# When a batch's router does its steps inside an attention unit: the gate products, one exponential, the last transposes

## The chip, the cores and the metric

The kernel runs on one core of one Trainium2 chip. The metric is the device time of one execution in microseconds (us). Before the change it is 1287.62 us, the median of three runs (1287.07 to 1288.91).

## The reference

Attention over 8 batches and 8 heads, whose queries are averaged in twos, and behind it a mixture of 8 experts, of which each token uses one.

```python
q_pool = q.reshape(8, 8, 576, 2, 64).mean(axis=3)           # q, k, v: (8, 8, 1152, 64)
scores = q_pool @ k.transpose(0, 1, 3, 2) / 8.0
attn = softmax(scores)                                      # 576 x 1152 for each head
x = (attn @ v).transpose(0, 2, 1, 3).reshape(4608, 512)
logits = x @ w_gate                                         # (4608, 8)
e_idx = argmax(logits, axis=1)
gate_w = softmax(logits)[e_idx]
eom = sigmoid(x @ w_output_gate)[e_idx]
out = gate_w * eom * (relu(x @ w1[e_idx]) @ w2[e_idx])      # w1: 512x1024, w2: 1024x512
```

## The kernel before

The attention works through 32 pairs, one pair being two heads of one batch, four pairs to a batch. A pair is cut into 11 units, named in `UNITS`: nine D units (two chunks of 128 keys against 512 queries) and two T units (numbers 4 and 10, the last 64 queries of one head against all keys). For each unit TensorE makes the scores (lines L396 and L397) into one of two PSUM tiles of two banks, `sps`. ScalarE exponentiates them twice: once into float16 (`ph`) and once into float32. The difference of the two, `pl`, is formed on GpSimd in the even units and on VectorE in the odd ones (L465), where the float32 exponential stands in `sps` itself. An odd unit's score tile is therefore free only when L465 has read it. Three units later TensorE multiplies `ph` and `pl` with the values (L479 to L481, tile `av`). Between these, TensorE makes products of the next pair's queries and keys (`mp`, L339; mostly two to a unit) whose row maxima VectorE reduces (`pm`, L341).

The `mp` products, the transposes and the router share three PSUM banks, handed out by `psum()`: the bank that has been free longest is next. A tile that asks with `hold` keeps its bank until `free`; meanwhile the `mp` products go round in two banks, and each has to wait until VectorE has read the one two before it.

The order on TensorE, VectorE, ScalarE and GpSimd is written out by hand; each engine does its instructions in the order in which the program issues them. The main loop issues a unit in this order: the pending L465 of the unit before; one step of every router generator (`step_routers(True)`); the unit's scores and their exponentials; then `mp` products and value products in turn. In units 2 and 8 of a pair, which `CLOSE` names by the unit whose values are due, three before (10 and 5), all value products come first, and behind them the normalisation of a finished head (`norm`, L520 to L522, which writes `xb`). Between the first and the second `mp` product of a D unit, `step_routers(False)` steps those generators again whose last yield was not a 1. So a `yield 1` says "next at the start of the next unit", and a bare `yield` says "next in the middle of this D unit, or at the start of the next unit, whichever comes first".

A router generator `logits(b, c, xb)` starts in unit 2 of the pair that follows the pair (b, c). It transposes the two heads' columns of `xb` on TensorE (L576) in two groups, of two and three blocks; ScalarE writes the float16 part `xTh` (L578), and VectorE the rest `xTl` (L580). For the last pair of a batch (c is 3) it goes on: `at(8)` yields 1 until unit 8, then come 60 small products with the gate weights (the burst, L591) into a held bank. `router` follows: two GpSimd iotas, the maximum and the expert's choice on VectorE (L607 to L611), then L615 and L617, the exponential of the logits on ScalarE (L619, tile `exg`), which frees the held bank, and `sums()`: a reduction on VectorE (L625), its exponential on ScalarE (L626) and another reduction (L630). From unit 2 of the next pair on the ranks and the scatter follow (L637 to L667).

A batch's router thus runs in the first pair of the next batch. There are seven such pairs, numbers 4, 8, 12, 16, 20, 24 and 28; they are called router pairs here, and the others ordinary pairs. The eighth batch's router runs behind the attention. "Unit 0" behind a router pair is that of the following pair. The experts' work (`Moe`, L1034 to L1107) comes after the attention.

Of the kernel before, what the change touches and what calls it, by code (L numbers as in the profile page):

```python
# [92 lines left out]
def attention(tc, qT, kT, vL, wg, keep, xrows, idscr, cum, pairs, setup, scat, init, exps, behind, presplit, lastav):  # L93
    nc = tc.nc
    nb = len(pairs) // 4
    with ExitStack() as ctx:
# [17 lines left out]
        def psum(hold=False, name="tp"):  # L114

            while len(held) == 3:
                pop() if fill else pendv.pop(0)()
            k = next(i for i in banks if i not in held)
            free(k)
            if hold:  # L120
                held.add(k)
            x = ps_m.tile([128, 512], F32, name=name, tag=f"mp{k}")
            return (x, k) if hold else x

        def free(k):
            held.discard(k)
            banks.remove(k)
            banks.append(k)
# [227 lines left out]
        def pop(k=1):  # L356
            while k and fill:
                fill.pop(0)()
                k -= 1
# [150 lines left out]
        def close(n, h):  # L510
            p = pairs[n]
            if p[0] not in xbs:
                xbs[p[0]] = sm.tile([128, 5, XW], F32, name="xb", bufs=2)
            xb = xbs[p[0]]
            av_ = avt[n, h][1]
            r = keep['rs'][:, 2 * n + h]
            H = 2 * p[1] + h

            def norm():
                nc.vector.tensor_scalar(out=r, in0=av_[:, :, 64], scalar1=1e-9 * math.exp(SHIFT), scalar2=VS / XS, op0=ALU.add, op1=ALU.mult)  # L520
                nc.vector.reciprocal(out=r, in_=r)
                nc.vector.tensor_tensor(out=xb[:, :, 64 * H:64 * H + 64], in0=av_[:, :, 0:64], in1=r.unsqueeze(2).broadcast_to([128, 5, 64]), op=ALU.mult)  # L522
                if h == 1:
                    routers.append([logits(p[0], p[1], xb), 0])
            fill.insert(0, norm)
# [4 lines left out]
        def at(k):  # L530
            while cur[0] != k:
                yield 1
# [34 lines left out]
        def logits(b, c, xb):  # L567

            yield 1
            if c < 3:  # L570
                yield 1
            for c0, c1, grp in ((0, 256, (0, 1)), (256, NQ, (2, 3, 4))):
                tx, tk = psum(True)
                for i, t in enumerate(grp):
                    r = 64 if t == 4 else 128
                    nc.tensor.transpose(out=tx[:, 128 * i:128 * i + r], in_=xb[0:r, t, 128 * c:128 * c + 128], identity=ident[0:r, 0:r])  # L576
                hi, lo = (x[:, c, c0:c1] for x in xT)
                nc.scalar.copy(out=hi, in_=tx[:, 0:c1 - c0])  # L578
                yield 1
                nc.vector.tensor_tensor(out=lo, in0=tx[:, 0:c1 - c0], in1=hi, op=ALU.subtract)  # L580
                free(tk)
            if c < 3:
                return
            if b < nb - 1:
                yield from at(8)
            pop(99)
            tl, tk = psum(True)
            ops = [(xT[i][:, c_], w[:, c_]) for c_ in range(4) for i, w in ((0, wh), (0, wl), (1, wh))]
            for t in range(5):
                for i, (x, w) in enumerate(ops):  # L590
                    mm = nc.tensor.matmul(tl[:, 16 * t:16 * t + 16], lhsT=x[:, 128 * t:128 * t + 128], rhs=w, start=i == 0, stop=i == len(ops) - 1)  # L591
            yield from router(b, xb, tl, tk, mm)
# [3 lines left out]
        def router(b, xb, tl, tk, lt):  # L596
# [18 lines left out]
            V.tensor_tensor(out=ohb, in0=em8, in1=b8(em), op=ALU.is_equal)  # L615
            so = sm.tile([128, 5, 8], F32, name="so", bufs=2)
            V.tensor_tensor(out=so, in0=og, in1=ohb, op=ALU.mult)  # L617
            ex = exg[b % 2]
            late.append(nc.scalar.activation(out=ex[:, :, 0:8], in_=g, func=AF.Exp, scale=1.0 / LSC))  # L619
            free(tk)  # L620
# [971 lines left out]
```

## Time and profile before

| | |
|---|---|
| Median of three runs | 1287.62 us |
| Profiled execution, its own time | 1290.03 us |
| Span of the program in that execution | 1288.2 us |
| Granted TensorE clock, mean | 0.996 |
| TensorE busy | 1214.6 us (94%) |
| VectorE busy | 1062.5 us (82%) |
| ScalarE busy | 1023.6 us (79%) |
| GpSimd busy | 856.8 us (67%) |

The profiled execution is 2.4 us above the median. Busy time is a sum over stages; the attention takes about the first 850 us of the span, the experts the rest. A busy TensorE is not one at its peak, since the ends of its matmuls are modelled.

### The profile page before, as it was taken

The numbers are of one execution on the slowest core, as the hardware profiler recorded it, in microseconds if no ns is written. First come the engines' busy times: TensorE is split into PE (matmuls) and PEld (weight loads), VectorE is DVE, ScalarE is ACT, GpSimd is POOL, SyncE is SP. The second block draws the span as 40 slices with busy tenths as digits, with TensorE's granted clock in tenths as the row PEclk, the third lists the DMA queues.
The fourth block names the chain that finished last, engine by engine and source line by source line (L and its number), as shares of the span: only waits on it lengthen the run. The fifth ranks groups of instructions, "written<-read, shape, count | busy, mean of one in ns | idle before, by whom it ended". The sixth has DMA issues, their size and how long they took to land.

```text
span 1288.2 us, 39248 instructions
## 1 busy us (share of the span) xinstructions
PE 1214.6 (94%) x15960; PEld 829.0 (64%) x15960; DVE 1062.5 (82%) x2149; ACT 1023.6 (79%) x1528; POOL 856.8 (67%) x709
## 2 busy tenths in 40 slices
PE   6999999899999999999999999899999999999996
PEld 3666656566666666666666666577676767666764
DVE  8898879788888888888888989887877676767886
ACT  6999889799899989989989889955656565656784
POOL 6988788789889879879879998536233333233421
PEclk9999999999999999999999999999999999999999
DMA  5455444345444445445545653079986767676850
GB/s 175 143 159 168 133 133 138 108 137 143 142 134 135 127 125 157 131 127 134 156 125 137 190 160 106 15 236 351 400 298 224 270 215 270 220 267 223 304 170 16
DMA packets 102209, 225.54 MB, mean 175 GB/s; under 512 B 18411, under 2 KB 33983, under 8 KB 102018
## 3 DMA queue, kind: packets, MB, share of 16 engines
q1 hardware_dynamic: 92114, 201.42, 49.8%
q0 software_dynamic: 9056, 20.85, 4.8%
q8 instruction: 127, 2.08, 0.7%
q10 hardware_dynamic: 848, 0.66, 0.2%
q14 instruction: 64, 0.52, 0.1%
HBM read 160.04 MB, written 22.50 MB: 142 GB/s over the span
## 4 chain that ended last, share of the span: by engine, by line
PE 55%; DVE 18%; ACT 12%; POOL 7%; issue 4%; DMA 3%; SPq 1%; ACTq 0%; DVEq 0%; POOLq 0%
PE hps L1053 14%; DVE pm L341 5%; PE sps L396 5%; PE yp L1092 5%; PE yp L1093 5%; PE sps L397 5%; DVE pl L465 5%; PE yp L1095 4%; PE mp L339 4%; ACT sps L461 4%; ACT ph L460 4%; PE av L481 3%; PE av L479 3%; PE av L480 3%; POOL pl L445 2%
## 5 line engine op out<-in xcount | busy, mean ns | idle before, releaser
L341 DVE TENSOR_REDUCE pm<-mp 128x1 f32<-128x512 f32 (+2 forms) x672 | 417.8, 663 | 28.3 <-PE mp L339 24.9
L445 POOL TENSOR_TENSOR pl<-p,ph 128x1024 f16<-128x1024 f32 x128 | 272.6, 2130 | 85.9 <-ACT ph L444 80.2
L396 PE MATMUL sps<-qa,ka 128*128 128x512 f16 (+2 forms) x1216 | 266.1, 280 | 8.0 <-DVE pl L465 7.3
L397 PE MATMUL sps<-qb,kb 65*128 65x512 f16 (+2 forms) x1216 | 266.8, 280 | 3.1 <-DMA qb<-mr 2.9
L479 PE MATMUL av<-vt,ph 128*128 128x65 f16 x2304 | 263.1, 193 | 3.3 <-DVE xb L522 3.2
L480 PE MATMUL av<-vt,ph 128*128 128x64 f16 x2304 | 263.6, 194 | 0.0
L481 PE MATMUL av<-vt,pl 128*128 128x65 f16 x2304 | 262.2, 193 | 1.1 <-issue 0.7
L479 PEld LDWEIGHTS <-ph 128*128 128x128 f16 x2304 | 215.4, 97 | 62.9 <-issue 24.0
L465 DVE TENSOR_TENSOR pl<-sps,ph 128x512 f16<-128x512 f32 x310 | 199.7, 686 | 61.2 <-ACT sps L461 54.8
L480 PEld LDWEIGHTS <-ph 128*128 128x128 f16 x2304 | 213.4, 97 | 40.3 <-issue 0.8
L339 PE MATMUL mp<-ka,qa 128*128 128x512 f16 (+1 forms) x768 | 203.9, 326 | 17.5 <-DVE pm L341 15.5
L481 PEld LDWEIGHTS <-pl 128*128 128x128 f16 x2304 | 214.0, 99 | 1.7 <-POOL pl L445 0.9
L1053 PE MATMUL hps<-x,w1h 128*128 128x256 f16 (+2 forms) x1408 | 207.1, 260 | 3.7 <-DVE x L1041 3.7
L1053 PE MATMUL hps<-x,w1l 128*128 128x256 f16 (+2 forms) x704 | 178.6, 260 | 0.0
L461 ACT ACTIVATE sps<-sps 128x1024 f32<-128x1024 f32 x155 | 159.8, 1031 | 1.0
L443 ACT ACTIVATE p<-sps 128x1024 f32<-128x1024 f32 (+1 forms) x160 | 140.8, 880 | 23.8 <-PE sps L397 14.6
L460 ACT ACTIVATE ph<-sps 128x1024 f16<-128x1024 f32 x124 | 128.1, 1033 | 23.4 <-PE sps L397 21.1
L1067 ACT ACTIVATE hh<-hps 128x512 f16<-128x512 f32 (+2 forms) x88 | 48.1, 548 | 119.4 <-PE hps L1053 118.1
L1053 PEld LDWEIGHTS <-w1h 128*128 128x128 f16 x1408 | 131.6, 98 | 15.4
L397 PEld LDWEIGHTS <-kb 65*128 65x128 f16 x1216 | 97.2, 97 | 58.6 <-issue 17.0
L444 ACT ACTIVATE ph<-sps 128x1024 f16<-128x1024 f32 x128 | 131.7, 1029 | 0.0
L396 PEld LDWEIGHTS <-ka 128*128 128x128 f16 x1216 | 98.3, 98 | 45.7 <-issue 3.9
(308 smaller groups left out, 2798.3 us busy)
## 6 DMA issues: line engine op xcount, KB each, us to landing
vp<-in_vL_dram SPq DMA_DIRECT2D x32, 576.0 KB
qp<-in_qT_dram SPq DMA_DIRECT2D x31, 576.0 KB
kpf<-in_kT_dram SPq DMA_DIRECT2D x31, 576.0 KB
ka<-xk SPq DMA_DIRECT2D x120, 144.0 KB
raw2a<-in_w_dram SPq DMA_DIRECT2D x16, 1024.0 KB
raw1b<-in_w_dram SPq DMA_DIRECT2D x14, 1024.0 KB
raw2b<-in_w_dram SPq DMA_DIRECT2D x14, 1024.0 KB
raw1c<-in_w_dram SPq DMA_DIRECT2D x14, 1024.0 KB
```

The costliest lines, as they stand in the source:

```text
L339: nc.tensor.matmul(mp[:, w * j:w * j + w], lhsT=l, rhs=r, start=True, stop=True)
L341: nc.vector.tensor_reduce(out=o, in_=mp[:, 0:w * len(ts)].rearrange("p (t k) -> p t k", t=len(ts)), axis=AX.X, op=ALU.max)
L396: for m in (nc.tensor.matmul(out, lhsT=st['ka'][:, h, ks], rhs=st['qa'][:, o + q0:o + q1], start=True, stop=False), nc.tensor.matmul(out, ...
L397: nc.tensor.matmul(out, lhsT=st['kb'][:, h, ks], rhs=st['qb'][:, h, q0:q1], start=False, stop=True)):
L445: nc.gpsimd.tensor_tensor(out=pl, in0=p32, in1=ph, op=ALU.subtract)
L460: ex(out=ph, in_=x)
L461: e_ = ex(out=x, in_=x)
L465: l = nc.vector.tensor_tensor(out=pl[:, j], in0=x[:, j], in1=ph[:, j], op=ALU.subtract)
L479: nc.tensor.matmul(o[:, 0:65], lhsT=hi, rhs=vt[:, h, c, 0:65], start=first, stop=False)
L480: nc.tensor.matmul(o[:, 0:64], lhsT=hi, rhs=vt[:, h, c, 66:130], start=False, stop=False)
L481: lastav[:] = [nc.tensor.matmul(o[:, 0:65], lhsT=lo, rhs=vt[:, h, c, 0:65], start=False, stop=last).ins]
L1053: d['mm'] = nc.tensor.matmul(hp[:, f, 0:w], lhsT=W1[l][g][:, c, fs], rhs=d['x'][:, c, o:o + w], start=c == 0 and i == 0, stop=c == 3 and i ...
```

## The change

Three lines are added to or altered in the two generators; all of them apply to the batches 0 to 6 only (`b < nb - 1`).

```diff
         def logits(b, c, xb):
             yield 1
-            if c < 3:
+            if c < 3 or b < nb - 1:
                 yield 1
...
             if b < nb - 1:
                 yield from at(8)
+                yield
             pop(99)
             tl, tk = psum(True)
...
             V.tensor_tensor(out=so, in0=og, in1=ohb, op=ALU.mult)
+            if b < nb - 1:
+                yield
             ex = exg[b % 2]
             late.append(nc.scalar.activation(out=ex[:, :, 0:8], in_=g, func=AF.Exp, scale=1.0 / LSC))
             free(tk)
```

The first puts the last pair's transposes of a batch at the starts of units 4 and 5, where those of the other three pairs are, in place of units 3 and 4. The second puts the burst and the two iotas in the middle of unit 8, between its two `mp` products and so behind its scores and value products, in place of its start. The steps behind it move along: L607 to L611 from the middle of unit 8 to the start of unit 9, L615 and L617 from the start to the middle of unit 9. The third puts L619 at the start of unit 10, behind unit 9's exponentials on ScalarE, in place of the start of unit 9. With it `sums()` (L625, L626, L630) goes from the middle of unit 9 to the start of unit 0 of the next pair, since unit 10 is a T unit and has no middle step. The ranks stay at unit 2.

## Rows read from the trace of the kernel before

**Rows 1.** The page, part 1: busy us, share of the span, instructions by engine.
```profile
PE 1214.6 (94%) x15960; PEld 829.0 (64%) x15960; DVE 1062.5 (82%) x2149; ACT 1023.6 (79%) x1528; POOL 856.8 (67%) x709
```
**Rows 2.** TensorE's waits, 100 to 840 us: total us, times, longest.
```profile
PE mp L339 <- DVE pm L341: 14.2, 31, 0.7
PE tp L576 <- DVE xb L522: 7.3, 7, 1.1
```
**Rows 3.** ScalarE's waits in the same stretch.
```profile
ACT exg L619 <- DVE so L617: 13.8, 7, 2.0
```
**Rows 4.** Stretches, ordinary and router pair: length, busy of PE, PEld, DVE, ACT, POOL, clock.
```profile
308.40:315.21 6.81, 6.76 (x120) 4.74 (x116) 6.21 (x13) 6.65 (x11) 5.55 (x5) 1.00 0.45 168
332.33:340.07 7.74, 6.69 (x119) 4.67 (x116) 6.06 (x12) 6.88 (x11) 6.30 (x6) 1.00 0.25 81
319.13:328.09 8.96, 8.58 (x150) 5.69 (x146) 8.36 (x19) 8.96 (x12) 7.74 (x6) 1.00 0.33 79
343.99:355.89 11.90, 10.29 (x209) 7.33 (x206) 9.26 (x26) 9.15 (x14) 7.63 (x7) 1.00 0.56 165
```
**Rows 5.** Timeline, TensorE, router pair 12: start, us, what, [idle before, releaser].
```profile
335.66 0.41 PE L576 MATMUL tp<-ident,xb 128*128 128x128 f32 x2 [1.05 <-DVE xb L522]
...
346.02 0.17 PE L591 MATMUL tp<-wh,xTh 128*128 128x16 f16 x1 [0.39 <-DVE pm L341]
...
347.53 0.38 PE L396 MATMUL sps<-qa,ka 128*128 128x512 f16 x1
...
351.35 0.38 PE L339 MATMUL mp<-ka,qa 128*128 128x512 f16 x1 [0.30 <-DVE pm L341]
...
352.76 0.38 PE L339 MATMUL mp<-ka,qa 128*128 128x512 f16 x1 [0.67 <-DVE pm L341]
...
355.89 0.38 PE L396 MATMUL sps<-qa,ka 128*128 128x512 f16 x1 [0.25 <-DVE pl L465]
```
**Rows 6.** Timeline, TensorE, ordinary pair 11 from unit 8 to unit 0.
```profile
321.04 0.38 PE L396 MATMUL sps<-qa,ka 128*128 128x512 f16 x1
...
323.10 0.59 PE L339 MATMUL mp<-ka,qa 128*128 128x512 f16 x2
323.53 0.38 PE L396 MATMUL sps<-qa,ka 128*128 128x512 f16 x1
...
327.50 0.39 PE L339 MATMUL mp<-ka,qa 128*128 128x128 f16 x4
...
328.09 0.38 PE L396 MATMUL sps<-qa,ka 128*128 128x512 f16 x1
```
**Rows 7.** Timeline, VectorE, units 8 to 10 of pair 11.
```profile
324.64 2.47 DVE L341 TENSOR_REDUCE pm<-mp 128x1 f32<-128x512 f32 x4
327.25 1.29 DVE L465 TENSOR_TENSOR pl<-sps,ph 128x512 f16<-128x512 f32 x2
```
**Rows 8.** Timeline, VectorE, unit 8's router steps in pair 12.
```profile
351.21 0.19 DVE L607 TENSOR_REDUCE mx<-tp 128x5 f32<-128x40 f32 x1
...
352.03 0.68 DVE L341 TENSOR_REDUCE pm<-mp 128x1 f32<-128x512 f32 x1
```
**Rows 9.** Timeline, ScalarE, units 9 and 10 of pair 12.
```profile
353.08 0.20 ACT L619 ACTIVATE exg<-tp 128x40 f32<-128x40 f32 x1 [1.97 <-DVE so L617]
353.18 1.02 ACT L460 ACTIVATE ph<-sps 128x1024 f16<-128x1024 f32 x1
...
355.02 0.20 ACT L626 ACTIVATE sl<-sl 128x5 f32<-128x5 f32 x1
```
**Rows 10.** Timeline, ScalarE, units 0 and 1 behind pair 11.
```profile
328.81 1.08 ACT L424 ACTIVATE p<-sps 128x512 f32<-128x512 f32 x2 [0.43 <-PE sps L397]
...
331.36 1.02 ACT L460 ACTIVATE ph<-sps 128x1024 f16<-128x1024 f32 x1 [0.56 <-PE sps L397]
```
**Rows 11.** Timeline, ScalarE and TensorE, units 4 and 5 of pair 6.
```profile
181.53 0.67 ACT L256 CAST xk<-kpf 128x576 f16<-128x576 f32 x1 [3.08 <-DMA kpf<-in_kT_dram]
...
185.09 0.50 PE L396 MATMUL sps<-qa,ka 128*128 128x512 f16 x1 [2.81 <-DVE pl L465]
```

## The prediction, made before the changed kernel ran

> **What bounds the kernel now.** I read the page first, then the waits of TensorE and ScalarE in the attention, then the lengths of matching stretches of a router pair and an ordinary pair, and last the timeline of both. The page has TensorE busy for 94% of the span, the other engines for 67% to 82% [rows 1]: time can be won only where TensorE stands still, or by taking work from it, and this change takes none. Its largest waits are `mp` products that wait for VectorE's maxima (14.2 us in 31 waits) and transposes that wait for `xb` (7.3 us in 7) [rows 2]. ScalarE waits 13.8 us for L617, also 7 times, once in each router pair [rows 3]. Seven is the number of router pairs.
>
> What this costs is seen in the stretches [rows 4]. From unit 2's first score product to unit 5's, ordinary pair 11 takes 6.81 us and router pair 12 takes 7.74, with the same TensorE work (6.76 and 6.69 busy): the same five transposes, standing elsewhere. From unit 7's first score product to unit 0's of the next pair they take 8.96 and 11.90 us. In pair 11's stretch TensorE is busy 8.58 of 8.96 us, so this is nearly its floor. The router's own TensorE work there is the burst, 346.02 to 347.53, that is 1.51 us [rows 5]. The excess is therefore 0.93 us in the first stretch and 11.90 - 8.96 - 1.51 = 1.43 us in the second, and the timeline shows where it lies: 1.05 us before the transposes, 0.39 before the burst, 0.30 and 0.67 before unit 9's `mp` products, 0.25 before unit 0's scores [rows 5].
>
> **The change part by part.** *Transposes a unit later.* They are moved to where the other three pairs have theirs; five transposes, two casts and two subtractions go along, all issued in the same order as there. `xb` is then written long before. Pair 11 is the picture of it, so the stretch should take 6.81: -0.93 us. No DMA is moved, and `at(8)` still finds the transposed data two units old.
>
> *Burst behind unit 8's scores.* I lay pair 11's times out from unit 8's first score product, t = 0 at 321.04 [rows 6], and put 1.51 us in. The first `mp` product stands at 2.06 and the second at about 2.3, so the burst runs from 2.3 to 3.8; unit 9's scores move from 2.49 to 4.00, unit 10's last `mp` product from 6.46 to 7.97, unit 0's scores from 7.05 to 8.56. Does anything then wait? VectorE starts the four maxima of units 8 and 9 at 3.60, 0.60 apart (2.47 us for four of 0.68) [rows 7]; the burst does not hold them, since the first needs only the product at 2.06. Unit 8's two are done at 4.88. L607 to L611 took 0.82 us from the first to the next maximum [rows 8], and are free to start, the burst being over: 4.80 to 5.62. Unit 9's first maximum runs to 6.30; L615 and L617, at the same 0.2 us each, to 6.63; unit 9's second to 7.31. Unit 9's scores are four products, 1.01 us by the 0.38 of one and the 0.59 of two [rows 6], and complete at 5.01; its two exponentials take 1.94 us on ScalarE (from L619 to L626) [rows 9], to 6.95. L465 can start at 7.23, VectorE's next turn, and its first half, half of 1.29 us, is read at 7.9. Unit 0's scores want that at 8.56: 0.65 us to spare. The bank that the burst holds is now held until unit 10, so the products of units 9 and 10 go round in two banks. Each needs the maximum two products before. Unit 9's first, four products of 0.21 behind 4.00, stands at 4.85 and needs the one that ends at 4.28: 0.57 us to spare. Unit 10's last, at 7.97, needs the one that ends at 7.31: 0.66. The two between have about 1 us. So the stretch should take 8.96 + 1.51 = 10.47: -1.43 us. The iotas are two short GpSimd instructions on an engine at 67%, wanted a pair later: nothing.
>
> *Exponential behind unit 9's.* L619 finds its input long there, and its 1.97 us of idle time [rows 9] goes. That time is not counted again: it is part of why L465, and with it unit 0's scores, came late.
>
> *`sums()` at unit 0.* This is the new wait, and the diff does not show it. L626 now stands on ScalarE ahead of unit 0's exponentials and waits for L625, which stands on VectorE behind both maxima of unit 10. VectorE: L465 until 8.52, the maxima until 9.72, L625 until 9.83. L626 runs at 9.87, the exponentials behind it from 9.97. Pair 11 has them 0.72 us behind the scores (328.81 against 328.09) [rows 6, 10], which would be 9.28. So 0.69 us of hold. Unit 1's exponentials, next on ScalarE, have 0.56 us of idle time before them in pair 11 [rows 10], which swallows most: 0.13 us is left, and passes through unit 1's L465 to unit 3. From below the cost is nothing; a gain is excluded, for no engine is given work earlier. From above I take a hold as long as L619's 1.97 us, and of the longest hold in the trace, 3.08 us on a late load, all but 0.27 us came out on TensorE (2.81) [rows 11]: 1.70 us. I take 0.13, since its terms are rows of just this place.
>
> *Sum.* Per router pair -0.93 - 1.43 + 0.13 = -2.23 us, and seven of them -15.6 us. The profiled execution took 1290.03 us, so its like after the change takes 1274.4. It lies 2.4 us above the median of the runs, and on the median of 1287.62 the sum gives **1272.0 us**. Behind the attention nothing is altered, so the experts start as much earlier as the attention ends.
>
> **The rivals.** *First: the hold at unit 0 takes back most of it.* VectorE is nearly always busy in units 8 to 10 (8.36 of 8.96 us even in pair 11 [rows 4]), and if it comes to L625 1.3 us later than I have it, the hold is as long as L619's and costs 1.70 us: -0.66 us a pair, 4.6 in all, 1283.0 us. Against it: the burst gives VectorE 1.51 us in which TensorE feeds it nothing. The Trainium skill ("TensorE: Matmul & The Clock Gate", under the engine queue depths) has ScalarE's and VectorE's queues as strictly first in, first out. The trace agrees: L460, whose scores were long there, ran right behind L619 and its 1.97 us [rows 9]. By that rule the hold cannot be passed; could it be, the sum would be 7 x 2.36 = 16.5 us less.
>
> *Second: the burst only changes its place.* The waits behind the burst [rows 5] come back in units 9 and 10, because VectorE still has the same eight small steps to fit in. Then only the transposes pay: -0.93 + 0.13 a pair, 5.6 in all, 1282.0 us. For it speaks that VectorE's work is the same; against it that these steps were pushed together before, because `norm` and unit 8's maxima had to wait for products that stood behind the burst; now the value products and the first `mp` product stand ahead of it.
>
> *Third, slower: the bank.* It is held from the middle of unit 8 to unit 10, so four `mp` products go round in two banks where two did. If VectorE runs 1.3 us later than laid out, each of the four waits as the worst did, 0.67 us [rows 5], and unit 0's scores wait their 0.25 again: 2.93 us a pair, against 2.23 won. That is +0.70 us, 4.9 in all, 1292.5 us. It decides from the point where the spare 0.57 us is used up, and makes the kernel slower once the four lose 2.23. Against it: two of the four have about 1 us to spare. The Trainium skill ("Trainium Kernel Development and Optimization", Best Practices) says that bubbles which recur can mean that PSUM ran out; the 0.30 and 0.67 in every router pair agree with it, and by it alone this change, which holds the bank longer, would lose.
>
> **How the numbers follow.** The forecast has 0.76, the first rival 0.10, the second 0.09, the third 0.05. The range is 1267 to 1282 us: its lower end is the sum without any hold (16.5 us, 1271.1) less some 4 us, since a late load as that of 3.08 us [rows 11] may fall elsewhere or nowhere; its upper end reaches to the second rival. What one measurement of this kernel can tell from no change is about 0.2%, 2.6 us: forecast and the first two rivals lie beyond it. Faster 0.93; within 0.2%, 0.03, from the near parts of the second and third; slower 0.04.
>
> **What would show it.** The waits of L576 for `xb` should be gone, and unit 2 to unit 5 take 6.8 us in router pairs. The burst should start behind unit 8's first `mp` product without a wait and unit 9's scores come 4.0 us behind unit 8's; L619 should have no idle time before it; unit 7 to unit 0 should take some 10.5 us. ScalarE should stand idle some 1.1 us before L626 (the 0.43 that pair 11 has there [rows 10] and the 0.69), and unit 1's exponentials should follow with almost no gap. I am wrong if L339 or unit 0's scores wait in units 9 and 10, if L626's idle time is near 2 us and unit 3's scores wait for L465, or if the seven pairs gain and the loads of the pairs behind them come later by as much.

## The result, and the profile after

The changed kernel took 1268.71 us (median of 4 runs, 1266.22 to 1271.5), the kernel before 1287.34 us in the same rounds (4 runs, 1284.13 to 1288.91). The ratio is 0.9858, with a 95% interval of 0.9839 to 0.9876: 18.6 us less, where 15.6 were forecast. The profiled execution took 1269.41 us; its span is 1267.7 us, against 1290.03 and 1288.2 before. Lines of the code up to 585 keep their numbers; the burst's L591 is now L592, L607 is L608, L617 is L618, L619 is L622, L625 and L626 are L628 and L629.

The page of the kernel after, part 1, against [rows 1]. TensorE's work is the same to 0.5% (1214.6 to 1209.3 us), its instructions the same in number; what went is time between them.

```profile
PE 1209.3 (95%) x15960; PEld 827.6 (65%) x15960; DVE 1060.0 (84%) x2149; ACT 1023.1 (81%) x1528; POOL 856.3 (68%) x709
```

The waits of the kernel after, 100 to 840 us (total, times, longest), against [rows 2, 3]:

```profile
PE mp L339 <- DVE pm L341: 9.3, 17, 0.8
...
ACT sl L629 <- DVE sl L628: 9.3, 7, 1.4
...
ACT xk L256 <- DMA kpf<-in_kT_dram: 3.4, 3, 1.6
...
ACT exg L622 <- DVE so L618: 2.8, 2, 2.4
...
PE sps L397 <- DMA qb<-mr: 1.5, 3, 0.8
```

The transposes' seven waits for `xb` are gone, 14 of the 31 waits of the `mp` products too. ScalarE's seven waits at the exponential of the logits are down to two, and seven new ones stand at L629, the second ScalarE step of `sums()`. The stretches of router pair 12, unit 2 to unit 5 and unit 7 to unit 0, as in [rows 4]:

```profile
321.30:328.10 6.80, 6.75 (x120) 4.73 (x116) 6.19 (x13) 6.64 (x11) 5.45 (x5) 1.00 0.25 89
332.02:342.11 10.09, 9.75 (x210) 7.20 (x207) 9.48 (x25) 9.25 (x13) 8.13 (x8) 1.00 0.42 93
```

7.74 became 6.80, and 11.90 became 10.09 us, 0.4 below the 10.47 forecast. TensorE's timeline of that router pair, units 8 to 10, and its only waits from unit 8's scores to unit 3 of the next pair, the two in the last lines:

```profile
333.94 0.38 PE L396 MATMUL sps<-qa,ka 128*128 128x512 f16 x1
...
336.00 0.38 PE L339 MATMUL mp<-ka,qa 128*128 128x512 f16 x1
336.21 0.17 PE L592 MATMUL tp<-wh,xTh 128*128 128x16 f16 x1
...
337.94 0.38 PE L396 MATMUL sps<-qa,ka 128*128 128x512 f16 x1
...
338.81 0.38 PE L339 MATMUL mp<-ka,qa 128*128 128x512 f16 x1
339.02 0.19 PE L479 MATMUL av<-vt,ph 128*128 128x65 f16 x1
...
339.36 0.19 PE L481 MATMUL av<-vt,pl 128*128 128x65 f16 x1
339.39 0.38 PE L339 MATMUL mp<-ka,qa 128*128 128x512 f16 x1
...
342.11 0.38 PE L396 MATMUL sps<-qa,ka 128*128 128x512 f16 x1
...
350.48 0.38 PE L339 MATMUL mp<-ka,qa 128*128 128x512 f16 x1 [0.82 <-DVE pm L341]
...
351.65 0.38 PE L339 MATMUL mp<-ka,qa 128*128 128x512 f16 x1 [0.43 <-DVE pm L341]
```

The burst starts 0.21 us behind unit 8's first `mp` product, without a wait; unit 9's scores come 4.00 us behind unit 8's (333.94 to 337.94). None of the five waits of [rows 5] is left; one that the kernel before does not have stands just ahead of unit 8's scores (told of at e1). ScalarE in the same place, and into the next pair:

```profile
340.92 0.20 ACT L622 ACTIVATE exg<-tp 128x40 f32<-128x40 f32 x1
...
343.69 0.21 ACT L629 ACTIVATE sl<-sl 128x5 f32<-128x5 f32 x1 [1.31 <-DVE sl L628]
343.81 1.07 ACT L424 ACTIVATE p<-sps 128x512 f32<-128x512 f32 x2
...
345.67 1.04 ACT L460 ACTIVATE ph<-sps 128x1024 f16<-128x1024 f32 x1
```

L622 has no idle time, where L619 had 1.97 [rows 9]. L629 stands idle 1.31 us ahead of unit 0's exponentials, forecast at some 1.1, and unit 1's (345.67) follow with no gap, where pair 11 had 0.56 [rows 10].

### The profile page after: what moved, and what is told of

Read it like the earlier page. It is cut to its first block, busy times and chain, and to the rows that moved or that the text cites. A ratio compares the mean times of both kernels' runs of the same rounds, so it can differ in the third digit from the quotient of the medians.

```text
span 1267.7 us, 39249 instructions
## 1 busy us (share of the span) xinstructions
PE 1209.3 (95%) x15960; PEld 827.6 (65%) x15960; DVE 1060.0 (84%) x2149; ACT 1023.1 (81%) x1528; POOL 856.3 (68%) x709
## 4 chain that ended last, share of the span: by engine, by line
PE 55%; DVE 18%; ACT 12%; POOL 8%; issue 5%; DMA 2%; SPq 1%; DVEq 0%; POOLq 0%; ACTq 0%
PE hps L1056 15%; PE yp L1095 5%; PE yp L1096 5%; PE sps L396 5%; DVE pm L341 5%; DVE pl L465 5%; PE yp L1098 4%; PE sps L397 4%; PE mp L339 4%; ACT sps L461 4%; ACT ph L460 4%; PE av L481 3%; PE av L480 3%; PE av L479 3%; ACT ph L444 2%
## 5 line engine op out<-in xcount | busy, mean ns | idle before, releaser
L341 DVE TENSOR_REDUCE pm<-mp 128x1 f32<-128x512 f32 (+2 forms) x672 | 416.2, 662 | 25.4 <-PE mp L339 24.2
L465 DVE TENSOR_TENSOR pl<-sps,ph 128x512 f16<-128x512 f32 x310 | 199.5, 685 | 53.5 <-ACT sps L461 49.6
```

What stands on the lines that cost most here:

```text
L341: nc.vector.tensor_reduce(out=o, in_=mp[:, 0:w * len(ts)].rearrange("p (t k) -> p t k", t=len(ts)), axis=AX.X, op=ALU.max)
L465: l = nc.vector.tensor_tensor(out=pl[:, j], in0=x[:, j], in1=ph[:, j], op=ALU.subtract)
```

## The experiments

Twelve kernels ran, each at least five times. The table has, for each, lengths between units' first score products in TensorE's timeline, the median over the six router pairs 4 to 24 (the seventh, pair 28, is told of further down). "Both" is the sum of the router pair's and the next pair's median, from which the last-but-one column is worked out: (both - 53.00) x 7 / 1288. The last is measured.

| kernel | unit 2 to 5 | unit 7 to 0 | router pair | next pair | both | share it would give | ratio, 95% |
|---|---|---|---|---|---|---|---|
| before | 7.75 | 11.90 | 27.80 | 25.20 | 53.00 | | |
| after | 6.81 | 10.08 | 25.05 | 25.23 | 50.28 | -1.5% | 0.9858, 0.9839 to 0.9876 |
| a_after (the same) | 6.80 | 10.08 | 25.05 | 25.24 | 50.29 | -1.5% | 0.9850, 0.9826 to 0.9873 |
| e1 transposes only | 6.80 | 12.25 | 27.22 | 25.28 | 52.50 | -0.3% | 1.0009, 0.9990 to 1.0028 |
| e2 burst only | 7.75 | 9.76 | 25.65 | 25.50 | 51.15 | -1.0% | 0.9906, 0.9881 to 0.9932 |
| e3 exponential only | 7.74 | 11.49 | 27.38 | 24.99 | 52.37 | -0.3% | 0.9954, 0.9933 to 0.9974 |
| e10 without the exponential | 6.81 | 10.07 | 25.04 | 25.13 | 50.16 | -1.5% | 0.9854, 0.9825 to 0.9883 |
| e11 without the transposes | 7.75 | 9.76 | 25.66 | 25.53 | 51.19 | -1.0% | 0.9912, 0.9886 to 0.9939 |
| e7 burst of 20 | 6.81 | 9.79 | 24.76 | 25.53 | 50.29 | -1.5% | 0.9855, 0.9833 to 0.9878 |
| e4 sums split | 6.81 | 10.08 | 25.05 | 24.88 | 49.93 | -1.7% | 0.9855, 0.9833 to 0.9877 |
| e5 bank held | 6.81 | 10.08 | 25.05 | 25.27 | 50.32 | -1.5% | 0.9873, 0.9852 to 0.9895 |
| e6 ranks at unit 6 | 6.81 | 10.07 | 25.04 | 25.02 | 50.06 | -1.6% | 0.9923, 0.9901 to 0.9944 |
| e8 rows later | 6.81 | 10.08 | 25.05 | 25.24 | 50.30 | -1.5% | 0.9843, 0.9814 to 0.9871 |
| e9 split, rows later | 6.81 | 10.07 | 25.04 | 24.87 | 49.92 | -1.7% | 0.9828, 0.9801 to 0.9855 |

The two last columns agree within the intervals but for e1 and e6; e4 lies at the edge of its interval. The edits below are against the kernel after.

**a_after: the kernel after, once more.**

> The changed kernel unaltered, as the yardstick for the other three. Time against the kernel before 0.986, as measured (0.984 to 0.988). In its trace unit 3 of the pair behind a router pair shows TensorE waits of 0.82 and 0.43 us before the mp products, and the exponential in sums() some 1.3 us of idle time before it.

1270.43 us (1266.28 to 1272.21): the same stretches to 0.01 us.

**e1, e2, e3: one edit of the three each.** e1 takes the second and the third out:

```diff
             if b < nb - 1:
                 yield from at(8)
-                yield
...
-            if b < nb - 1:
-                yield
             ex = exg[b % 2]
```

e2 leaves out the first (`if c < 3:` again) and the third, e3 the first and the second.

> The kernel before with the first edit alone (the last pair's transposes a unit later). Theory (the parts add up, each by the wait that it takes away): unit 2 to unit 5 of a router pair 6.8 us instead of 7.74, unit 7 to unit 0 still 11.9; 7 x 0.93 = 6.5 us off, 0.995 of the kernel before. Rival (the time only moves on to the burst, which then waits longer): unit 7 to unit 0 grows, less than 2 us off.

> The kernel before with the second edit alone (the burst in the middle of unit 8); the exponential of the logits then comes in the middle of unit 9, sums() at the start of unit 10. Theory (what pays is that the burst stands behind the value products, so that norm and the maxima are done beside it): unit 7 to unit 0 falls from 11.90 to 10.1, unit 2 to unit 5 stays 7.74; 7 x 1.8 = 12.6 us off, 0.990; the exponential in sums() waits some 1 us at unit 10. Rival (the third edit is what pays, by the 1.97 us of idle time on ScalarE): the stretch stays over 11 us, less than 6 us off.

> The kernel before with the third edit alone: the exponential of the logits in the middle of unit 9, behind unit 9's exponentials, sums() at the start of unit 10. Theory (TensorE's waits of 0.30 and 0.67 us in unit 9 are VectorE's, only the 0.25 at unit 0's scores and the rest of their delay come from the hold on ScalarE): ScalarE's 1.97 us go, TensorE's waits in unit 9 stay, unit 7 to unit 0 falls from 11.90 to some 11.5; 2 to 3 us off, 0.998. Rival (the hold on ScalarE is the main cost): the stretch falls below 10.7 us, more than 8 us off.

e1 (1289.77 us) has its 6.80 in units 2 to 5, but units 7 to 0 grew from 11.90 to 12.25. TensorE's waits there, in e1's timeline:

```profile
341.76 0.27 PE L375 MATMUL tp<-ident,m 128*5 128x128 f32 x1 [0.34 <-DVE pm L341]
...
342.35 0.17 PE L591 MATMUL tp<-wh,xTh 128*128 128x16 f16 x1 [0.32 <-DVE pm L341]
...
347.68 0.38 PE L339 MATMUL mp<-ka,qa 128*128 128x512 f16 x1 [0.30 <-DVE pm L341]
...
349.09 0.38 PE L339 MATMUL mp<-ka,qa 128*128 128x512 f16 x1 [0.67 <-DVE pm L341]
...
352.22 0.38 PE L396 MATMUL sps<-qa,ka 128*128 128x512 f16 x1 [0.24 <-DVE pl L465]
```

The four waits from the burst to unit 0 stand as in [rows 5]; the first, 0.34 us, the kernel before does not have, and a third of the gain is lost in it. It comes with the first edit, in the kernel after too. There VectorE has, and TensorE behind it:

```profile
332.30 0.48 DVE L580 TENSOR_TENSOR xTl<-tp,xTh 128x320 f16<-128x320 f32 x1
```

```profile
333.83 0.27 PE L375 MATMUL tp<-ident,m 128*5 128x128 f32 x1 [0.34 <-DVE pm L341]
```

The second subtraction of the transposes, L580, moves with them: before it ran in unit 5 (341.21), now it runs 0.27 us behind unit 7's scores, ahead of the maxima L341 whose bank L375 takes (what L375 reads, the result of L348, was done at 333.18). All nine of these kernels that have the first edit have this wait at L375 (0.33 or 0.34 us in pair 12), and the four without it have none there; pair 11, an ordinary one, has it too (0.33 us at 320.93).

The 0.50 us that remain of "both" would be 3.5 us in all; none was measured, and by the interval it is at most 1.3 us. A part of it goes at unit 0 of the next pair: in e1's profile its scores wait for the copies `qb` in five of the six pairs, 0.08 to 0.65 us, in the kernel before in one. With each router pair added to its own next pair, the median gain is 0.31 us. In e1's profile 3.4 us came back in the pairs behind the next ones (their sum is 180.9 us, before 177.5), whose loads come late at times, and 1.9 us behind the attention (473.4 us from the last pair's first score product to the end, before 471.5); whether that is so in each run was not measured.

e2 (1277.13 us) is the theory's ratio. Its unit 7 to unit 0 is even 0.3 us below that of all three, since it does not have the wait at L375, but the next pair 0.3 us above. e3 (1284.55 us) gave 5.5 us, over the 2 to 3 that its theory had: 0.41 us in units 7 to 0, as expected, and 0.2 in the next pair, which was not expected.

**e10, e11: the change without one edit.** e10 takes the third out, e11 the first.

> Edits one and two of the change without the third: the transposes a unit later, the burst behind unit 8's scores, the exponential of the logits where it stood, ahead of unit 9's exponentials. Theory of the prediction (the idle time ahead of the exponential is a part of the burst's wait and is not counted again): the exponential finds its logits late again in unit 9, and sums() moves back to unit 10, so that the wait at unit 0 goes. Router pairs 24.7 to 25.1 us, next pairs 24.9 instead of 25.2; 0.983 to 0.986 of before, no worse than all three. Rival (the medians add: -0.1, -0.9 and -0.5%): without the third edit the time is about 0.990.

> Edits two and three of the change without the first: the transposes stay a unit earlier and wait for xb. Theory of the prediction: router pairs 25.05 + 0.93 = 25.98 us, unit 2 to unit 5 7.74 and unit 7 to unit 0 10.08; 6.5 us more than all three, about 0.990 of before. Rival (the transposes alone left the time at 1.001, since what they win is waited for again elsewhere): unit 7 to unit 0 falls to 9.7 as in the burst alone, router pairs 25.6, and the time is within 3 us of the kernel after, 0.986 to 0.987.

e10 (1271.95 us) cannot be told from the kernel after: the third edit is worth nothing beside the others. The theory gave the time right and its place wrong. ScalarE's timeline of e10, unit 0's scores of the next pair being at 346.05:

```profile
344.86 0.20 ACT L620 ACTIVATE exg<-tp 128x40 f32<-128x40 f32 x1
346.45 0.21 ACT L627 ACTIVATE sl<-sl 128x5 f32<-128x5 f32 x1 [1.39 <-DVE sl L626]
346.56 0.63 ACT L443 ACTIVATE p<-sps 128x576 f32<-128x576 f32 x1
```

The exponential is not late: the second edit had moved it behind unit 9's exponentials already, with all that follows the burst. What the third edit moves is `sums()`, from ahead of unit 10's exponentials to ahead of unit 0's; ScalarE waits 1.39 us there, 1.31 here, and the later place costs the next pair some 0.1 us (25.13 to 25.23).

e11 (1278.79 us) shows the transposes at nearly their full price: "both" is 0.91 us longer than with them, 6.4 us in all, and the time 7 to 8 us. The theory has the time right, the rival the place: units 7 to 0 take 9.76 us and the router pair 25.66, for the wait at L375 is gone, so that the transposes win 0.61 us of the router pair and not 0.93. The other 0.30 is in the next pair (25.53 to 25.23), in units 0 and 3. That they win nothing in the whole falls for the change; it holds for the transposes alone.

**e7: a burst of 20 products.** The kernel leaves out the two correction products of each three, so that its logits are rounded more coarsely.

```diff
-for i, w in ((0, wh), (0, wl), (1, wh))]
+for i, w in ((0, wh), (0, wl), (1, wh))[:1 if b < nb - 1 else 3]]
```

> The changed kernel with a burst of 20 products instead of 60 (the two products with the low-order parts are left out, so the logits are less exact), 0.50 us instead of 1.51. Theory (the burst costs its full length on TensorE, except that the first 0.40 us of it stand where TensorE would else wait for norm before unit 9's value products): unit 8 to unit 9 falls from 4.00 to 2.99, unit 9 to unit 10 stays 2.39, 7 x 1.0 = 7 us off the changed kernel, 0.980 of the kernel before. Rival (VectorE's small steps set the pace in units 9 and 10, the burst gives them time): part of the 1.0 comes back as waits before mp products and before unit 0's scores, unit 8 to unit 0 falls by less than 0.6.

1270.56 us, the rival's. TensorE has 1.0 us less to do in units 8 to 10, and 0.29 of it shows at unit 0 (10.08 to 9.79), all of which the next pair gives back (25.23 to 25.53). The reason can be read from VectorE's timeline. The kernel after, from unit 7's L465, which VectorE does beside unit 8, to the first step of `sums()`:

```profile
335.33 1.29 DVE L465 TENSOR_TENSOR pl<-sps,ph 128x512 f16<-128x512 f32 x2 [0.37 <-ACT sps L461]
...
337.55 1.28 DVE L341 TENSOR_REDUCE pm<-mp 128x1 f32<-128x512 f32 x2
...
341.08 1.28 DVE L465 TENSOR_TENSOR pl<-sps,ph 128x512 f16<-128x512 f32 x2
342.28 1.28 DVE L341 TENSOR_REDUCE pm<-mp 128x1 f32<-128x512 f32 x2
343.48 0.18 DVE L628 TENSOR_REDUCE sl<-so 128x5 f32<-128x40 f32 x1
```

and e7, whose router pair starts 0.11 us earlier:

```profile
335.23 1.29 DVE L465 TENSOR_TENSOR pl<-sps,ph 128x512 f16<-128x512 f32 x2 [0.36 <-ACT sps L461]
...
337.44 1.28 DVE L341 TENSOR_REDUCE pm<-mp 128x1 f32<-128x512 f32 x2
...
340.98 1.28 DVE L465 TENSOR_TENSOR pl<-sps,ph 128x512 f16<-128x512 f32 x2
342.17 1.28 DVE L341 TENSOR_REDUCE pm<-mp 128x1 f32<-128x512 f32 x2
343.37 0.18 DVE L628 TENSOR_REDUCE sl<-so 128x5 f32<-128x40 f32 x1
```

Each step stands 0.10 or 0.11 us earlier, as the whole pair does: VectorE runs through from 335.33 to 343.66 with no wait marked, with 60 products or with 20. So behind the change it is VectorE that sets the pace from unit 8 on, as far as these timelines show, and TensorE's 1.51 us of burst lie beside it for the most part.

**e4: the sums split.** The first reduction (L628) runs at the start of unit 0, the exponential and the second reduction a step later, so that nothing on ScalarE waits for VectorE ahead of unit 0's exponentials.

```diff
                 V.tensor_reduce(out=sl, in_=so, axis=AX.X, op=ALU.add)
+                yield
                 e_ = nc.scalar.activation(out=sl, in_=sl, func=AF.Exp, scale=-1.0 / LSC)
...
             if b < nb - 1:
-                sums()
+                g_ = sums()
+                next(g_)
+                yield
+                next(g_, None)
                 yield from at(2)
```

> The changed kernel, but of sums() only the reduction L625 stays at the start of unit 0; its exponential and the second reduction come in the middle of unit 0, behind unit 0's exponentials. Theory (the hold on ScalarE at unit 0 passes through unit 1's L465 to unit 3): the 1.31 us of idle time before the exponential goes, the wait of 0.82 us in unit 3 falls back to the 0.50 of the kernel before, unit 3 to unit 4 from 3.9 to some 3.55 us, and the time falls by 7 x 0.33 = 2.3 us, to 0.998 of the changed kernel. Rival (unit 3 waits for the rank's small VectorE steps, the hold is slack): the idle time goes, unit 3 still takes 3.9, the time stays.

In the stretch it is as the theory had it: the next pair falls from 25.23 to 24.88, the wait for L629 is gone from ScalarE, and unit 3's `mp` product waits 0.50 instead of 0.82. That is the cost of the hold, 0.35 us. But the time, 1271.97 us, did not fall; late loads took it back in the profile, which shows the longest of its five runs (1274.32 us). ScalarE's and TensorE's timelines of e4, pair 6:

```profile
179.28 0.67 ACT L256 CAST xk<-kpf 128x576 f16<-128x576 f32 x1 [3.00 <-DMA kpf<-in_kT_dram]
```

```profile
182.84 0.59 PE L396 MATMUL sps<-qa,ka 128*128 128x512 f16 x1 [2.71 <-DVE pl L465]
```

It is the wait of [rows 11] in the same pair; in the two profiles of the kernel after, pair 6 had none of it (24.7 us, in e4 29.7, before 28.3). From 100 to 840 us e4's waits for these key loads add up to 6.9 us in 6, the kernel after's to 3.4 in 3.

**e5: the bank held for longer,** to unit 1 of the next pair.

```diff
-            free(tk)
+            if b == nb - 1:
+                free(tk)
...
+                yield from at(1)
+                free(tk)
```

> The changed kernel, but the bank of the logits is given back at the start of unit 1 instead of unit 10. Theory of the bank (two banks cost nothing as long as VectorE's maximum of two products before is done, with 0.6 us to spare in units 9 and 10, and none in unit 0): no new wait in unit 10; in unit 0 the transpose of the maxima needs the bank of unit 0's first product, whose maximum ends some 2.4 us behind unit 0's scores, where it would start at 2.0: a wait of 0.3 to 0.5 us, unit 0 to unit 1 from 2.14 to some 2.5 us, and 2 to 3.5 us in all. Rival (the bank is never what is waited for): no new wait, the time of the changed kernel.

1272.87 us (1272.37 to 1274.69). The interval of its ratio overlaps that of the kernel after, but all five runs lie above the five of a_after, by 2.4 us at the medians, as the theory had it. "Both" does not show this (50.32 against 50.29); e5's profile has longer waits for the key loads (8.1 us in 6, the kernel after 3.4 in 3), and whether the bank causes them was not tried. TensorE's timeline at unit 1 of the next pair:

```profile
347.50 0.27 PE L375 MATMUL tp<-ident,m 128*4 128x128 f32 x1 [0.18 <-DVE pm L341]
```

Unit 0 grew by 0.39 us (2.14 to 2.53), as expected, and unit 3 gave it back (3.90 to 3.54): the same work of VectorE is waited for at another place. Units 9 and 10, where the third rival had its waits, have none. The Trainium skill ("Trainium Kernel Development and Optimization", Best Practices) says that recurring bubbles can mean that SBUF or PSUM ran out. The 0.30 and 0.67 us of [rows 5] agree with it in so far as these products wait for a bank that VectorE has still to read, and so does e5's 0.18 us. But how long the bank is held does not by itself make them: the change holds it longer and e5 longer still, and neither has a wait in units 9 and 10. What a further bank would do was not tried.

**e6: e4's split, and the ranks at unit 6 instead of unit 2.**

```diff
-                yield from at(2)
+                yield from at(6)
```

> As the kernel with sums() split, and the ranks start in unit 6 instead of unit 2 of the pair behind a router pair, with the scatter behind them. Theory (the waits of 0.50 and 0.43 us in unit 3 come from a bank held just when VectorE has L465 and norm to do): unit 3 to unit 4 falls from 3.55 to some 2.6 us, and if units 6 and 7 have room on VectorE the time falls by up to 7 x 0.93 = 6.5 us against the kernel with sums() split. Rival (VectorE has no room in unit 6 either, and the held bank makes the transpose of the maxima in unit 7 wait): what unit 3 gives is taken in units 6 and 7, and the time is within 2 us of that kernel's.

1280.72 us, 10 us more than the kernel after, though "both" is shorter than the kernel after's. In the next pair theory and rival are both half right: unit 3 falls to 2.59 us, as the theory said, but unit 6 grows from 1.88 to 3.06, as the rival said, where e6 has a wait that none of the other kernels has:

```profile
PE mp L339 <- DVE xTl L580: 7.2, 7, 1.0
```

The 10 us neither foresaw. The ranks set when the rows are scattered and written; TensorE's waits for one kind of DMA, the copies that build `qb`, in e6 (the kernel after has 1.5, 3, 0.8):

```profile
PE sps L397 <- DMA qb<-mr: 12.2, 9, 3.2
```

With the scatters and writes moved by four units, the copies that unit 0 of the pair two further on needs came late: it took 3.6 to 6.5 us in pairs 7, 15, 19 and 23, in the kernel after 2.2 to 2.6. Which of the moved transfers delayed them was not tried.

**e8, e9: the writes of the rows behind the key load,** for the kernel after and for e4.

```diff
-                with tc.issue_after(lastv[0].ins) if b < nb - 1 else ExitStack():
+                with tc.issue_after(lastk[0].ins) if b < nb - 1 else ExitStack():
...
-                if b < nb - 1:
+            if b < nb - 1:
+                yield from at(2)
+                for t in range(5):
                     wr(t)
```

> The kernel after, with one step moved: the five writes of a router pair's rows to xrows (each 256.5 KB but the last) are no longer issued one by one behind the five scatters, where three of them stand in the SP queue directly ahead of the loads for the pair after next (in the trace of the kernel after: three writes at 165.96, the two loads at 168.59 and 169.22, and unit 3 of pairs 6, 14, ... may then wait for them); they are issued together from unit 2 of the next pair but one, behind that pair's key load. Theory (what the medians leave over against the sum of the stretches is how late these loads land): the waits for these loads in pairs 6, 10, ..., 30 become short and steady, the seven pairs behind the next pair take 24.7 to 24.8 us each instead of 24.7 to 29.4, and the time falls by 2 to 4 us, to about 0.982 of before. Rival (the writes only push other loads): the value or query loads of the pair after that wait as with the ranks at unit 6 (units 0 of 3.6 to 6.5 us), and the time is the same or up to 10 us more.

> The kernel with the sums split (exponential and second reduction in the middle of unit 0, expectation e4), and with the writes of the rows issued together behind the key load as well. Theory (the 0.33 us of the wait at unit 0 is real, and late loads took it back in the split kernel): with steady loads it is 2 to 2.5 us less than the run with the rows later alone, about 0.980 of before. Rival (VectorE's and ScalarE's work, not the wait, sets the pace behind unit 0): the next pair shortens to 24.9 us, and what it gains comes back in the pair after it or as waits in units 4 to 6; no difference between the two.

The DMA queue of SyncE in the kernel after, and in e8:

```profile
166.16 2.58 SPq L662 DMA_DIRECT2D xrows<-xb  x3
168.78 0.59 SPq L177 DMA_DIRECT2D qp<-in_qT_dram  x1
169.41 0.44 SPq L178 DMA_DIRECT2D kpf<-in_kT_dram  x1
```

```profile
166.20 1.53 SPq L177 DMA_DIRECT2D qp<-in_qT_dram  x1
167.77 0.43 SPq L178 DMA_DIRECT2D kpf<-in_kT_dram  x1
168.30 4.37 SPq L662 DMA_DIRECT2D xrows<-xb  x5
```

e8 waits no more for the key loads at all, and for `qb` instead:

```profile
PE sps L397 <- DMA qb<-mr: 6.9, 6, 1.9
```

Theory and rival each have half: the writes changed what they push, and 1268.44 us cannot be told from the kernel after; three of the pairs behind the next ones still take 25.8 to 27.3 us. e9 (1266.08 us, 1265.38 to 1269.31) has the next pair at 24.87 and lies 2.4 us below e8, as the theory said; the intervals of the two overlap, and that of e9 overlaps the kernel after's. It is the fastest version that ran; against the kernel before its gain is 1.72%, by the interval 1.45 to 1.99%.

## Why the prediction was right, point by point

*Transposes (-0.93).* Right in the stretch (6.81) and, with the burst moved, in the whole (e11: 0.91). Not seen: they bring the wait of 0.34 us at L375 in unit 7, alone (e1) and with the burst. The layout had it in it unseen, since pair 11's 8.96 us hold it. Alone, they win nothing that was measured.

*Burst (-1.43).* The mechanism was right, the term too small: -1.82, since unit 7 to unit 0 is 10.08 and not 10.47. (The burst's own worth there is 2.14, by e2, 11.90 to 9.76; 0.32 goes to the wait at L375.) I laid out pair 11 and put 1.51 us into it, and so kept an idle time of pair 11 that the burst covers. TensorE in unit 9 of pair 11, kernel before:

```profile
324.40 0.38 PE L339 MATMUL mp<-ka,qa 128*128 128x512 f16 x1
324.78 0.20 PE L479 MATMUL av<-vt,ph 128*128 128x65 f16 x1
...
325.13 0.19 PE L481 MATMUL av<-vt,pl 128*128 128x65 f16 x1
325.37 0.38 PE L339 MATMUL mp<-ka,qa 128*128 128x512 f16 x1
```

The value products follow the `mp` product at 0.38 us and the next `mp` product follows them at 0.24; in the router pair after the change the same steps take 0.21 and 0.03 (338.81 to 339.02, 339.36 to 339.39). That is 0.38 us. Such small gaps carry no mark in the timeline, and 8.58 busy of 8.96 [rows 4] counted nearly all of it as busy; of the 0.38 us that are not, 0.33 are the wait at L375. I had called that "nearly its floor"; it was not.

*No new waits in units 9 and 10.* Right: the margins of 0.57 to 0.66 us sufficed, the second and third rivals are out, and e7 shows what would bring the second in: a burst shorter by 1.0 us makes one `mp` product wait and gains nothing.

*The hold at unit 0 (+0.13).* VectorE's L628 was done 9.72 us behind unit 8's scores (343.66 against 333.94), laid out at 9.83, and the exponentials ran at 9.87, laid out at 9.97. But unit 0's scores came 0.39 us early, so the hold is 343.81 - 342.11 - 0.72 = 0.98 us and not 0.69, and it cost 0.35 (e4) and not 0.13. The two errors hang together: VectorE's steps stayed nearly where they were laid out, and of the 0.39 us that TensorE gained in unit 9 it gave back 0.22 at unit 3. Without the third edit (e10) ScalarE's wait stands ahead of unit 10's exponentials and the two pairs are 0.12 us shorter, so the edit that brings the hold wins nothing here. The Trainium skill ("TensorE: Matmul & The Clock Gate", under the engine queue depths) has ScalarE's queue as strictly first in, first out; the traces agree, for unit 0's exponentials stood behind L629 in the kernel after, and waited 0.43 us for the scores alone in e4, as in [rows 10]. The first rival's mechanism is real, its price of 1.70 is not: 0.56 us of the 0.98 vanish in the gap before unit 1, which leaves 0.42 where 0.35 was measured, and of L629's 1.31 us of idle time 0.43 is there in any pair.

*Not in the sum.* Without the hold the next pair is 24.88, 0.32 us below that of before, and I had counted the router pair alone. Half of it is unit 0, whose scores no longer come late there (2.30 to 2.14); the other half is unit 10 (1.79 to 2.38 before, 1.77 or 1.78 after), and its cause is open. Per router pair it is then -0.94 - 1.82 - 0.32 + 0.35 = -2.73 us against -2.23. Six of them make 16.4; the seventh gave only 1.05 (router and next pair 53.87 to 52.82), since in pair 28 ScalarE stood 1.73 us at a cast (`xq`, L269) and unit 8's scores 1.24 us behind it. One profile of the kernel after has this cast wait for GpSimd, the other, for the same 1.73 us, for the copy `ka`; which it was stays open. Together 17.4 us, where 18.6 were measured (16.0 to 20.7 by the interval). The parts missed have both signs, so that the sum came nearer than they did, which is luck.

*Loads.* That late loads would fall elsewhere was in the range only, and rightly: pair 26 took 29.40 us in one profile of the kernel after and 26.42 in the other. Five runs of the kernel after (a_after) lie 5.9 us apart, and gains as those of e1 and e4 are lost in that.

## What to carry to other kernels

When a moved piece of work is laid out on the timeline of a stretch that does not have it, look for the small gaps in that stretch that the piece will cover, and ask which engine's steps stay in place: here VectorE's did, and most of what TensorE won beyond them came back at its next wait. An edit's worth hangs on the others (the transposes 0 alone and 7 to 8 us with the burst, the exponential 5.5 us alone and 0 with it), so take one out of the whole as well as trying each alone. And before moving a step that ends in DMAs, look at which loads stand behind them in the queue: two moves that shortened the stretches here (e4, e6) lost it to late loads in their profiles.

## What was not expected of the hardware

A matmul stream of 1.51 us could be cut to a third of its products with no effect on the time (e7), while VectorE's sequence beside it kept its times to 0.01 us. Three writes ahead of two loads in one queue moved the issue of the key load by 1.6 us (169.41 against 167.77 us), and in one profile each the waits went from `kpf` (3.4 us in 3) to `qb` (6.9 us in 6) when they were turned round.
